# Cluster attention and a PReLU FFN on one core: copies of the queries' clusters, the table of weight conversions, and the turn back of the last batch are moved

## The chip, the cores and the metric

The kernel runs on one core of one Trainium2 chip. The time is device time in microseconds (us). A core has five engines that work side by side, each on its own queue in order: TensorE (PE, matmuls; its weight loads are PEld), VectorE (DVE), ScalarE (ACT), GpSimd (POOL) and SyncE (SP). Transfers (DMA) are issued by a queue, here mostly SP's, some by ScalarE's and GpSimd's, and then run by themselves. An instruction waits on semaphores that other engines or transfers raise.

## The reference

There are 4 batches of 8 heads with 768 tokens of 64 numbers. Each head has 16 centroids. Every query and every key goes to the centroid with which it has the largest cosine, and a query sees only keys of its own cluster. The result is put side by side over the heads and goes through a feed-forward network (FFN) of width 2048.

```python
q_assign = np.argmax(np.einsum('bhsd,hcd->bhsc', q_n, c_n), axis=-1)
k_assign = np.argmax(np.einsum('bhsd,hcd->bhsc', k_n, c_n), axis=-1)
mask = q_assign[:, :, :, None] == k_assign[:, :, None, :]
scores = np.where(mask, scale * np.matmul(q, k.transpose(0, 1, 3, 2)), -1000000000.0)
attn = softmax(scores)                       # over the keys
x = np.matmul(attn, v)                       # (B,H,S,D) -> (B*S, H*D), 3072 x 512
h = x @ w_in                                 # 512 x 2048
out = (np.maximum(h, 0.0) + alpha * np.minimum(h, 0.0)) @ w_out
```

The inputs q, k, v and the centroids are 32-bit floats; the weights of the FFN come to the chip as 64-bit floats, so the kernel converts them.

## The kernel before

**Tiles and steps.** Two heads are worked together as a pair; with four batches there are 16 pairs, pair n being heads 2hp and 2hp+1 of batch b, where n = 4b + hp. The 768 queries of a batch are cut into two halves of 384. In batches 0 to 2 the work of one pair and one half takes three steps, each with two blocks of 128 keys: so a batch has 24 steps, the first 12 for half 0 of its four pairs, the next 12 for half 1. The last batch (pairs 12 to 15) is sorted by cluster first and then needs only blocks near the diagonal.

**The order is written out by hand.** The loops over steps `u` emit the instructions of all engines, and each engine runs its own in that order. A step has five slots; `tick()` (L98) goes to the next slot and emits what `later(slots, piece)` (L95) had put there. Pieces can also be bound to a step and a slot through `at(step, slot, piece)` inside the loop that starts at L1072, run by `prepare(u, i)`. In slot 0 of a step come the scores and their exps (`score`, L735), in slot 1 the weighing with v (`weigh`) and the normalisation of a half that has ended; in slots 2 to 4 come FFN pieces (from step 12 on), preparations of later pairs, and one weight conversion per slot as long as `i < converting` (L1166). FFN pieces of a batch's half are fed in while the next half's attention runs.

**Clusters of batch 0.** For pair n, three steps ahead of its half 0, `prep_sims` multiplies features with centroids on TensorE, and `prep_argmax` (L414) makes on VectorE a one-hot table: the tile `member`, in which partitions 0 to 31 hold queries of half 0, 32 to 63 queries of half 1, and 64 to 127 the keys; a row is one of 2 x 16 clusters, a column a token. Seven slots later (twelve for pair 0) `of_heads` (L424) turns the keys' part into two masks, one per head, with two ScalarE passes (L426): a row of the head's own cluster becomes 0 for a key in it and -2^60 for others; rows of the other head become 0. Head 1's is written beside, head 0's in place of the one-hot table, so head 1's has to come first. In slot 2 of the step ahead of a half, `prep_queries` (L458) brings the queries' part to the partitions of the keys, into `aq`: by two copies on VectorE for the very first half (L469), and else by two transfers that ScalarE's queue issues (L471). In `score` two matmuls per head add mask times queries onto the scores (L763), head 0's first.

**Other work of ScalarE and VectorE in batch 0.** `prep_features` copies transposed features from PSUM to `qkT` on ScalarE (L358), three copies per pair, in the step ahead of `prep_sims`. The denominators of half 0 are summed by TensorE in one PSUM bank (L883); VectorE turns them (L896), inverts and spreads them (L902, L906, L865), and L990 writes the normalised result into `xT`, which frees the one PSUM bank of the weighing. L1014 is the first FFN matmul, over four channels, one for each pair's `xT`; L1032 is the second.

**Conversions.** There are 32, in four groups of four tiles of `w_in` and four of `w_out`, each of 128 x 512 numbers. `convert` (L244) issues the load into one of five raw buffers on SP's queue (L247) and gives three pieces. `split` is two VectorE instructions (L253, L255); four slots later `scale` is two on ScalarE (L259, L261); two slots later `join` is two on VectorE (L265, L268) and a product on GpSimd (L271). The tile `power` has three buffers. A raw buffer is loaded again when its join is done.

**The last batch's end.** `normalise_near` (L926) writes a pair's result in cluster order; it is turned to rows (L952, copied by ScalarE at L955), scattered back to token order by 12 indirect transfers that GpSimd issues (L960), and fetched by four transfers of SP (L972). Four slots after that has been issued, `turn_back` (L977) transposes the fetched rows into `xT` on VectorE (L982). Row sums of a pair's exps are made by additions (L815, L818), a turn (L824) and a sum (L832) on VectorE; L845 adds the parts up on TensorE. L795 applies masks on VectorE. L1006 is the slope of the PReLU on VectorE, after ScalarE's copy L1020. L696 and L702 prepare the next pair.

Of the kernel before, what the change touches and what calls it, by code (L numbers as in the profile page):

```python
# [11 lines left out]
BF16 = mybir.dt.bfloat16  # L12
# [3 lines left out]
AF = mybir.ActivationFunctionType  # L16
# [3 lines left out]
P = 128  # L20
# [3 lines left out]
def kernel(  # L24
# [11 lines left out]
    nc = tc.nc  # L36
# [5 lines left out]
    NCH = DM // P  # L42
    NF = DF // P
    HJ = NJ // 2
    HS = HJ * P
# [49 lines left out]
    def later(slots, piece):  # L95
        due.setdefault(now[0] + slots, []).append(piece)
# [317 lines left out]
    def prep_argmax(n, ps):  # L414
        top, first, pieces = argmax(ps, exact=n < NCH)
        for piece in pieces:
            piece()
        firsts[n] = first
        if n >= NCH:
            return  # L420
        member = memp.tile([P, 2, HS], BF16, name="member")
        nc.vector.transpose(out=member[:, 0, :], in_=top.rearrange("p t c -> p (t c)"))

        def of_heads():  # L424
            for h in (1, 0):
                nc.scalar.activation(  # L426
                    out=member[HP:P, h, :], in_=member[HP:P, 0, :], func=AF.Identity,
                    scale=pick[HP:P, h:h + 1], bias=pick[HP:P, h + 2:h + 3])

        members[n] = member  # L430
        later(12 if n == 0 else 7, of_heads)

    def prep_clusters(n):


        first = firsts.pop(n)
        ps = misc()
        for g in range(NG):
            nc.tensor.matmul(out=ps[:, g * 2 * NX:(g + 1) * 2 * NX], lhsT=spread[:, g, :],
                             rhs=first, start=True, stop=True)  # L440
        every = fsp.tile([P, NG, GT, NG, 2], BF16, name="every")
        everys[n] = every
        later(1, lambda: nc.scalar.copy(every.rearrange("p g i r h -> p (g i r h)"),
                                        ps[:, 0:NG * 2 * NX]))
        later(2, lambda: prep_keys(n))
# [12 lines left out]
    def prep_queries(n, half, h):  # L458

        if h == 0:  # L460
            aqs[n, half] = aqp.tile([P, 2, HS], BF16, name="aq")
        if n < NCH:

            if h == 0:
                r = slice(half * Q, (half + 1) * Q)
                for g in range(NG // 2, NG):
                    to = aqs[n, half][g * Q:(g + 1) * Q, 0, :]
                    if n == 0 and half == 0:
                        nc.vector.tensor_copy(out=to, in_=members[n][r, 0, :])  # L469
                    else:  # L470
                        nc.scalar.dma_start(out=to, in_=members[n][r, 0, :])  # L471
            return
        own_half = everys[n].rearrange("p g i r h -> p g (i r) h")[:, half, :, h:h + 1]
        nc.vector.transpose(out=aqs[n, half][:, h, :],
                            in_=own_half.broadcast_to((P, NX, Q)))
# [259 lines left out]
    def score(n, half, chunks, alone=None):  # L735


        qkT = qkTs[n]
        pss = [[ps_f.tile([P, 512], FP32, name="fps") for h in range(2)] if c == alone else
               ps_s.tile([P, 2, 512], FP32, name="sps") for c in chunks]  # L740
        early_mask = n < NCH

        def bank(ps, h, m=HS):
            return (ps[h] if isinstance(ps, list) else ps[:, h, :])[:, 0:m]

        def queries(c):
            lo, hi = ((half * HJ, (half + 1) * HJ) if half is not None else window(c))
            return slice(lo * P, hi * P), (hi - lo) * P

        for c, ps in zip(chunks, pss):  # L750
            tokens, m = queries(c)
            for h in range(2):
                r = h * D
                nc.tensor.matmul(  # L754
                    out=bank(ps, h, m),
                    lhsT=qkT[r:r + D, S + c * P:S + (c + 1) * P],
                    rhs=qkT[r:r + D, tokens], start=True, stop=not early_mask)
        if early_mask:
            for h in range(2):
                for c, ps in zip(chunks, pss):  # L760
                    g, i = divmod(NJ + c, GT)
                    r = slice(g * Q, (g + 1) * Q)
                    nc.tensor.matmul(  # L763
                        out=bank(ps, h), lhsT=members[n][r, h, i * P:(i + 1) * P],
                        rhs=aqs[n, half][r, 0, :], start=False, stop=True)
        for c, ps in zip(chunks, pss):
            E = e_tiles[0]
            e_tiles.append(e_tiles.pop(0))
            _, m = queries(c)
            if c == alone:  # L770
                for h in range(2):
                    nc.scalar.activation(out=E[:, h, 0:m], in_=ps[h][:, 0:m], func=AF.Exp,
                                         scale=SCALE)
            else:
                nc.scalar.activation(out=E[:, :, 0:m], in_=ps[:, :, 0:m], func=AF.Exp,  # L775
                                     scale=SCALE)
            waiting.append((n, half, c, E))
# [187 lines left out]
    def fetch_back(n, whole):  # L965

        b, hp = pairs[n]
        raw = inp.tile([P, 2, NJ, D], FP32, name="qk").rearrange("p h j d -> p (h j d)")
        for h in range(2):
            for x in range(D // Q):  # L970
                r = h * D + x * Q
                nc.sync.dma_start(  # L972
                    out=raw[r:r + Q, :].rearrange("p (t i) -> p t i", i=Q),
                    in_=whole[h * S:(h + 1) * S, x * Q:(x + 1) * Q].rearrange(
                        "(t p) i -> p t i", p=Q))

        def turn_back():  # L977
            for half in range(2):
                if (b, half) not in xTs:
                    pool = sorts["xmore"] if half else xpool  # L980
                    xTs[b, half] = pool.tile([P, NCH, HS], FP32, name="xT")
                nc.vector.transpose(out=xTs[b, half][:, hp, :],  # L982
                                    in_=raw[:, half * HS:(half + 1) * HS])
        later(4, turn_back)

    def normalise(n, half):
        b, hp = pairs[n]
# [84 lines left out]
    for (n, half), u in start_of.items():  # L1072
        def at(step, slot, piece):
            prep_at.setdefault((step, slot), []).append(piece)
        if half is None:
            t = ORDERS[n - NO]
            load_at.setdefault(t, []).append(lambda n=n: load(n))
            for i in range(2):
                at(t + 2, 2 + 2 * i, lambda n=n, i=i: order_features(n, i))
            at(t + 3, FIRST + 1, lambda n=n: order_sims(n))  # L1080
            at(t + 7, 2, lambda n=n: order_begins(n))
            load_at.setdefault(u - 4, []).append(lambda n=n: order_load(n))
            at(u - 4, 0, lambda n=n: prep_clusters(n))
            for i in range(2):
                at(u - 1, i, lambda n=n, i=i: order_blocks(n, i))
                at(u - 1, FIRST + i, lambda n=n, i=i: order_queries(n, i))
            continue
        if half == 0:
            if n < NCH:
                if n > 1:  # L1090
                    load_at.setdefault(max(u - 7, 0), []).append(lambda n=n: load(n))
                if n > 0:
                    load_at.setdefault(max(u - 6, 0), []).append(lambda n=n: load_v(n))
            else:
                load_at.setdefault(u - 9, []).append(lambda n=n: load(n))
                load_at.setdefault(u - 7, []).append(lambda n=n: load_v(n))
            if n < NCH:
                for g in range(len(groups)):
                    at(u - 4, FIRST + g, lambda n=n, g=g: prep_features(n, g))
            else:  # L1100
                for w in range(2):
                    at(u - 7, FIRST + w, lambda n=n, w=w: prep_blocks(n, w))
            at(u - (3 if n < NCH else 5 if u - 6 < TOGETHER else 6), FIRST,
               lambda n=n: prep_sims(n))
            if n >= NCH:
                at(u - 4, FIRST if u - 4 < TOGETHER else 0, lambda n=n: prep_clusters(n))
        for h in range(2):
            at(u - 1, FIRST + h, lambda n=n, half=half, h=h: prep_queries(n, half, h))

# [21 lines left out]
    for u in range(-AHEAD, TOGETHER):  # L1131
# [31 lines left out]
            feed_block(u)  # L1163
            whole = len(ffn) - KEEP
        take = (max(len(ffn) - KEEP - whole * (UB - 1 - u % UB) // UB, 0) if ffn else 0)
        converting = 0 if u < 0 else 2 if u < 2 else 1 + (u % 4 == 3) if u < UB else 2  # L1166
        for i in range(SLOTS - FIRST):
            tick()
            feed(take * (i + 1) // 3 - take * i // 3)
# [302 lines left out]
```

## Time and profile before

| what | value |
|---|---|
| median of 10 runs | 997.42 us (995.98 to 997.84) |
| profiled execution | 997.28 us |
| its span, first to last instruction | 995.4 us |
| TensorE busy | 970.3 us, 97% |
| VectorE busy | 634.4 us, 64% |
| up to 85.75 us: TensorE, VectorE, ScalarE busy | 75.45, 65.09, 52.87 us |
| 734.5 to 760.2 us: TensorE, VectorE busy | 22.12, 16.60 us of 25.70 |
| mean granted TensorE clock | 0.995 |

Batch 0's half 0 (steps 0 to 11) lasts to about 85.75 us, where the FFN begins beside the attention. In the views of the profile a row of a timeline is: start in us, length in us, engine, line, operation, what it writes `<-` what it reads, shapes, and how many instructions were merged; a bracket at its end gives the time for which its engine was idle before it and what ended that. The page's rows by slices cut the span into 40 equal parts, with the busy share of each in tenths. A table by stretch gives the length, then the busy time of PE, PEld, DVE, ACT and POOL (with instructions), the granted TensorE clock, the share of the DMA engines and GB/s.

### The profile page before, as it was taken

The page shows a single profiled execution, that of the slowest core. Times are in us where ns is not written, and L with a number is a line of the kernel's source. Part 1 is how long each engine was busy: PE and PEld are TensorE (multiplying, and loading weights), DVE is VectorE, ACT ScalarE, POOL GpSimd, SP SyncE. Part 2 cuts the span into 40 slices and gives each one's busy share as a digit, 9 for nine tenths or more (in the row PEclk, how much of TensorE's full clock was granted, in tenths as well). Part 3 has the DMA queues.
Part 4 walks back from the last instruction along what each step waited for, and adds up shares of the span by engine and source line. Part 5 has one row for each costly group of instructions (what it writes and reads, how often), then busy time and mean ns, then how long its engine had stood idle before and what let it go on. Part 6 is the DMA issues. An engine that isn't in the chain of part 4 may idle for free.

```text
span 995.4 us, 10857 instructions
## 1 busy us (share of the span) xinstructions
PE 970.3 (97%) x3947; PEld 481.3 (48%) x3947; DVE 634.4 (64%) x1143; ACT 258.3 (26%) x468; POOL 213.1 (21%) x249
## 2 busy tenths in 40 slices
PE   8899999999999999999999999999998999999997
PEld 5434444445454454545445454454554545455453
DVE  5887788598587776877857698678977522021010
ACT  5655443222121221212222022231222101010110
POOL 2322222010000635401000273620154440000000
PEclk9989999999999999999999999999999999999999
DMA  6533665042200362416020121811621120000000
GB/s 251 192 117 108 138 130 78 17 90 21 33 1 26 102 100 55 80 44 102 1 33 0 53 80 37 149 32 23 95 47 30 31 53 11 0 9 25 0 1 35
DMA packets 174285, 60.45 MB, mean 61 GB/s; under 512 B 161216, under 2 KB 164752, under 8 KB 174224
## 3 DMA queue, kind: packets, MB, share of 16 engines
q1 hardware_dynamic: 168768, 51.42, 24.2%
q0 software_dynamic: 4608, 7.87, 2.5%
q8 instruction: 33, 0.54, 0.2%
q10 hardware_dynamic: 848, 0.39, 0.2%
q14 instruction: 28, 0.23, 0.1%
HBM read 45.15 MB, written 14.16 MB: 60 GB/s over the span
## 4 chain that ended last, share of the span: by engine, by line
PE 90%; DVE 5%; ACT 2%; DMA 1%; issue 1%; POOL 0%; ACTq 0%; SPq 0%; DVEq 0%; POOLq 0%
PE fps L1014 32%; PE fps L1032 32%; PE vps L890 9%; PE sps L754 8%; PE fps L754 3%; PE sps L763 1%; PE mps L381 1%; ACT E L775 1%; DVE acc L824 1%; PE vps L923 1%; ACT member L426 1%; PE mps L923 1%; DVE gT L1006 1%; PE fps L883 0%; ACT power L259 0%
## 5 line engine op out<-in xcount | busy, mean ns | idle before, releaser
L1014 PE MATMUL fps<-xT,w_in_sb 128*128 128x384 f32 x1024 | 343.4, 491 | 2.7 <-ACT gT L1020 2.0
L1032 PE MATMUL fps<-w_out_sb,gT 128*128 128x512 f32 x768 | 341.2, 598 | 1.7 <-DVE gT L1006 1.7
L1014 PEld LDWEIGHTS fps<-xT,w_in_sb 128*128 128x128 f32 x1024 | 190.7, 190 | 142.8 <-ACT more L775 4.4
L1032 PEld LDWEIGHTS fps<-w_out_sb,gT 128*128 128x128 f32 x768 | 143.9, 191 | 174.3 <-issue 162.3
L660 POOL DMA_INDIRECT scratch<-stage,off x96 | 101.0, 1052 | 324.4 <-DMA stage<-in_v_dram 267.2
L1006 DVE SCALAR_TENSOR_TENSOR gT<-gT,alpha 128x384 f32<-128x384 f32 x128 | 80.8, 637 | 138.6 <-ACT gT L1020 138.3
L1020 ACT COPY gT<-fps 128x384 f32<-128x384 f32 x128 | 61.2, 478 | 337.8 <-PE fps L1014 335.7
L754 PE MATMUL sps<-qkT 64*128 64x384 f32 (+1 forms) x512 | 97.8, 501 | 0.6 <-ACT E L775 0.6
L795 DVE SCALAR_TENSOR_TENSOR more<-aq,key,more 128x384 f32<-128x384 bf16 (+1 forms) x136 | 74.4, 606 | 29.3 <-ACT more L775 19.0
L775 ACT ACTIVATE E<-sps 128x768 f32<-128x768 f32 (+1 forms) x81 | 61.2, 802 | 77.0 <-PE sps L763 45.7
L960 POOL DMA_INDIRECT back<-rows,place x48 | 49.6, 1034 | 103.6 <-ACT rows L955 90.2
L754 PEld LDWEIGHTS sps<-qkT 64*128 64x128 f32 x512 | 46.3, 189 | 46.4 <-issue 18.3
L890 PE MATMUL vps<-E,vt 128*64 128x384 f32 x356 | 67.0, 502 | 0.0
L795 DVE SCALAR_TENSOR_TENSOR E<-aq,key,E 128x384 f32<-128x384 bf16 (+1 forms) x104 | 56.5, 602 | 16.1 <-ACT E L775 11.4
L1040 DVE TENSOR_TENSOR y<-y,fps 128x512 f32<-128x512 f32 x30 | 20.6, 685 | 70.0 <-PE fps L1032 70.0
L805 DVE TENSOR_TENSOR acc<-acc,E 128x768 f32<-128x768 f32 x47 | 44.9, 956 | 16.9 <-ACT E L775 15.6
L1038 ACT COPY y<-fps 128x512 f32<-128x512 f32 x24 | 14.1, 586 | 144.2 <-PE fps L1032 144.2
L775 ACT ACTIVATE more<-sps 128x768 f32<-128x768 f32 (+1 forms) x47 | 35.4, 797 | 41.2 <-PE sps L754 40.8
L890 PEld LDWEIGHTS vps<-E,vt 128*64 128x64 f32 x356 | 23.3, 138 | 32.4 <-issue 31.7
L890 PE MATMUL vps<-more,vt 128*64 128x384 f32 x220 | 38.8, 491 | 0.0
L271 POOL TENSOR_TENSOR w_in_sb<-w_in_sb,power 128x512 f32<-128x512 f32 x16 | 22.2, 1385 | 71.1 <-DVE w_in_sb L268 71.1
L754 PE MATMUL fps<-qkT 64*128 64x384 f32 x160 | 34.5, 508 | 0.0
(177 smaller groups left out, 708.1 us busy)
## 6 DMA issues: line engine op xcount, KB each, us to landing
raw<-in_moe_w_in_dram SPq DMA_DIRECT2D x16, 512.0 KB, 4.2
raw<-in_moe_w_out_dram SPq DMA_DIRECT2D x16, 512.0 KB, 3.7
out_dram<-y SPq DMA_DIRECT2D x24, 256.0 KB, 2.1
vt<-in_v_dram SPq DMA_DIRECT2D x12, 384.0 KB, 4.3
qk<-in_q_dram SPq DMA_DIRECT2D x48, 96.0 KB, 3.5
qk<-in_k_dram SPq DMA_DIRECT2D x48, 96.0 KB, 3.5
qk<-scratch SPq DMA_DIRECT2D x32, 96.0 KB, 3.5
qk<-in_q_dram SPq DMA_DIRECT2D x4, 384.0 KB, 3.9
```

Of the source, the lines that this page charges most:

```text
L271: nc.gpsimd.tensor_tensor(out=dst, in0=dst, in1=power[0].bitcast(FP32), op=ALU.mult)
L660: nc.gpsimd.indirect_dma_start(out=scratch[n][1][h * NX + xx], out_offset=bass.IndirectOffsetOnAxis(ap=ranks[n][:, xx, h:h + 1], axis=0), ...
L754: nc.tensor.matmul(out=bank(ps, h, m), lhsT=qkT[r:r + D, S + c * P:S + (c + 1) * P], rhs=qkT[r:r + D, tokens], start=True, stop=not early_ ...
L775: nc.scalar.activation(out=E[:, :, 0:m], in_=ps[:, :, 0:m], func=AF.Exp, scale=SCALE)
L795: nc.vector.scalar_tensor_tensor(out=e, in0=of, scalar=keys[n][:, NJ + c, h:h + 1], in1=e, op0=ALU.is_equal, op1=ALU.mult)
L805: nc.vector.tensor_tensor(out=acc, in0=acc if first is None else first[3], in1=E, op=ALU.add)
L890: nc.tensor.matmul(out=po[r:r + D, 0:HS], lhsT=vts[n][:, h, c, :], rhs=e[:, h, :], start=(c == 0), stop=(c == NJ - 1))
L960: nc.gpsimd.indirect_dma_start(out=to[i], out_offset=bass.IndirectOffsetOnAxis(ap=place[:, h, j:j + 1], axis=0), in_=rows[:, j, h * D:(h + ...
L1006: nc.vector.scalar_tensor_tensor(out=gs[f], in0=gs[f], scalar=alpha[:, f:f + 1], in1=gs[f], op0=ALU.mult, op1=ALU.max)
L1014: nc.tensor.matmul(out=ps[:, 0:HS], lhsT=w_in_sb[:, c, f * P:(f + 1) * P], rhs=xTs[b, half][:, c, :], start=(c == 0), stop=(c == NCH - 1))
L1020: nc.scalar.copy(gs[f], ps[:, 0:HS])
L1032: nc.tensor.matmul(out=ps[:, 0:DM], lhsT=gs[f][:, i * P:(i + 1) * P], rhs=w_out_sb[:, f, :], start=on and f == f0, stop=off and f == f0 + ...
```

## The change

The one-hot table and the masks get tiles of their own: `member` keeps all of the table, and the two ScalarE passes write to a new tile `outside`, head 0 first. For pairs 1 to 3, the copies of half 0's queries are issued by `of_heads` itself, ahead of the two passes, at the start of the step before the half instead of in its slot 2. The copies of half 1 are issued three steps ahead of it instead of one. How many conversions begin in a step, which was 2, 2 and then 1, 2, 1, 1, 1, 2, 1, 1, 1, 2 for steps 0 to 11, comes from a table: 2, 0, 2, 2, 0, 2, 2, 1, 1, 1, 2, 2; the sum is 17 in both. `turn_back` follows nine slots after the fetch instead of four, but for the last pair.

```diff
-        member = memp.tile([P, 2, HS], BF16, name="member")
-        nc.vector.transpose(out=member[:, 0, :], in_=top.rearrange("p t c -> p (t c)"))
+        member = memp.tile([P, HS], BF16, name="member")
+        outside = memp.tile([P, 2, HS], BF16, name="outside")
+        nc.vector.transpose(out=member, in_=top.rearrange("p t c -> p (t c)"))

         def of_heads():
-            for h in (1, 0):
+            if n > 0:
+                prep_queries(n, 0, 0)
+            for h in range(2):
                 nc.scalar.activation(
-                    out=member[HP:P, h, :], in_=member[HP:P, 0, :], func=AF.Identity,
+                    out=outside[HP:P, h, :], in_=member[HP:P, :], func=AF.Identity,
                     scale=pick[HP:P, h:h + 1], bias=pick[HP:P, h + 2:h + 3])

-        members[n] = member
+        members[n] = member, outside
         later(12 if n == 0 else 7, of_heads)
...
                     if n == 0 and half == 0:
-                        nc.vector.tensor_copy(out=to, in_=members[n][r, 0, :])
+                        nc.vector.tensor_copy(out=to, in_=members[n][0][r, :])
                     else:
-                        nc.scalar.dma_start(out=to, in_=members[n][r, 0, :])
+                        nc.scalar.dma_start(out=to, in_=members[n][0][r, :])
...
-                        out=bank(ps, h), lhsT=members[n][r, h, i * P:(i + 1) * P],
+                        out=bank(ps, h), lhsT=members[n][1][r, h, i * P:(i + 1) * P],
...
-        later(4, turn_back)
+        later(4 if n == NP - 1 else 9, turn_back)
...
+        if n < NCH:
+
+            if half == 1 or n == 0:
+                at(u - (3 if half else 1), FIRST,
+                   lambda n=n, half=half: prep_queries(n, half, 0))
+            continue
         for h in range(2):
             at(u - 1, FIRST + h, lambda n=n, half=half, h=h: prep_queries(n, half, h))
...
-        converting = 0 if u < 0 else 2 if u < 2 else 1 + (u % 4 == 3) if u < UB else 2
+
+        converting = 0 if u < 0 else (2, 0, 2, 2, 0, 2, 2, 1, 1, 1, 2, 2)[u] if u < UB else 2
```

## The prediction

> **What bounds the kernel now.** The page first. TensorE is busy for 97% of a span of 995.4 us, so time can come only from its idle places, and the row of slices (40, digits in tenths) shows two: the first twelfth of the span, and a dent near 750 us.
>
> ```profile
> PE 970.3 (97%) x3947; PEld 481.3 (48%) x3947; DVE 634.4 (64%) x1143; ACT 258.3 (26%) x468; POOL 213.1 (21%) x249
> ...
> PE   8899999999999999999999999999998999999997
> ```
>
> Second, TensorE's timeline, where the square bracket is the idle time before a row and its releaser.
>
> ```profile
> 29.64 1.09 PE L354 MATMUL fps<-ident,qk 128*64 128x128 f32 x16 [1.76 <-ACT qkT L358]
> ...
> 48.65 1.21 PE L354 MATMUL fps<-ident,qk 128*64 128x128 f32 x16 [2.94 <-ACT qkT L358]
> ...
> 65.17 1.62 PE L754 MATMUL sps<-qkT 64*128 64x384 f32 x8 [0.60 <-ACT E L775]
> ...
> 68.48 0.85 PE L763 MATMUL sps<-aq,member 32*128 32x384 bf16 x4 [1.70 <-DMA aq<-member]
> ...
> 747.03 1.98 PE L1032 MATMUL fps<-w_out_sb,gT 128*128 128x512 f32 x4 [0.56 <-DVE gT L1006]
> 751.23 0.42 PE L845 MATMUL mps<-parts,fold 128*128 128x48 f32 x2 [2.21 <-DVE parts L832]
> 751.49 8.79 PE L1032 MATMUL fps<-w_out_sb,gT 128*128 128x512 f32 x16
> ```
>
> After the start-up (its last wait, 1.24 us, ends at 16.32) batch 0 has four waits: 1.76+2.94+0.60+1.70 = 7.00 us. The FFN's first L1014 begins at 85.75. The late dent has two: 0.56+2.21 = 2.77 us. Third, tables by stretch for the granted clock (the column before the DMA share):
>
> ```profile
> 49.50:53.00 3.50, 3.50 (x18) 1.31 (x13) 0.53 (x1) 0.58 (x1) 1.26 (x1) 0.51 0.58 211
> ...
> 70.00:73.40 3.40, 3.40 (x14) 1.27 (x12) 3.02 (x10) 1.86 (x4) 1.29 (x2) 0.50 0.80 263
> ...
> 752.60:756.10 3.50, 3.50 (x5) 1.35 (x5) 3.45 (x7) 0.00 (x0) 2.65 (x3) 0.51 0.10 33
> ```
>
> Behind three of the waits TensorE runs some 3.4 us at half clock, so each such wait costs about 1.7 us more. Last, VectorE's timeline in both places:
>
> ```profile
> 25.72 0.45 DVE L253 TENSOR_SCALAR power<-raw 128x512 uint32<-128x512 uint32 x1 [1.40 <-POOL w_in_sb L271]
> ...
> 31.57 1.76 DVE L268 SCALAR_TENSOR_TENSOR w_in_sb<-raw,w_in_sb 128x512 f32<-128x512 uint32 x1
> ...
> 739.40 1.04 DVE L982 STREAM_TRANSPOSE xT<-qk 128x384 f32<-128x384 f32 x2 [4.86 <-DMA qk<-back]
> ```
>
> At 739.40 the whole VectorE queue stood 4.86 us behind a turn back whose rows had not landed. The first row is a split that waits for GpSimd to free its power buffer; the second a join that takes 1.76 us instead of 0.69 because GpSimd's L271 runs from 31.13. The row that ends batch 0's half 0 on VectorE is L990 at 86.76, 0.56 long; the first FFN matmuls need its tile.
>
> **Turn back later.** For pairs 12, 13 and 14 the two transposes go five slots later in VectorE's queue; pair 15's stay. Nothing else on VectorE changes order there, and TensorE's and GpSimd's orders are the same throughout. For pair 12 the rows after the old place go on at 734.54 (end of the masks before it): two masks 1.02, two more 0.79, one slope 0.53 give 736.9; sums, turn and row sums of side 0 last 3.67 (742.70 to 746.37 now), giving 740.55; two slopes 1.05, whose second input ScalarE has by 740.63, give 741.6; three additions 1.79 give 743.4. Only now come the transposes: 0.96, to 744.4. Their data landed at 739.28, so they have 4.1 us to spare. Turn and row sums, 1.97, end at 746.3 instead of 751.18. TensorE's L1032 matmuls end at 746.47 and the slope they waited for is ready at 741.6: the 0.56 goes. The next four end at 748.5, L845's input is ready at 746.3: the 2.21 goes. The half clock goes with them: sixteen L1032 took 8.63 us on the chain against 6.97 at full clock elsewhere (167.60), 1.66. Sum 4.43 us. What is late next is ScalarE's copy of the hidden tile, waits of 0.24 to 0.57 that are there now too. Bounds: 2.2 if the clock or the 0.56 stays, 4.43 if all goes; I take 4.4, because the spare times are 2 to 5 us. Pair 13's transposes do not wait now (768.27); pair 14's 4.71 us at 791.25 is followed by slopes alone, and TensorE waits there only 0.24 and 0.57 for ScalarE: nothing gained. Who waits for the moved transposes? Only the last FFN blocks, from 824.8 us: nothing lost. SP's and GpSimd's queues are not passed by anything here; pair 13's scatter runs from 741.28 to 757.6 on GpSimd, with its gather about 7 us behind, before its new place near 772.
>
> [...]
>
> **The batch 0 edits.** Their order by engine: on ScalarE the copy pairs (0.5 to 0.6 us of issue each) move ahead of the two mask passes, pair 1's past six compute rows; four copies of half 1 come two steps earlier. No scale stands any more ahead of pair 2's three feature copies at 29.02, for step 1 has no conversions: that wait, 1.76, goes. SP issues pair 3's q and k ahead of two weight loads instead of behind: earlier, hidden. The separate mask tile lets head 0's matmuls start after one pass of 0.71, but head 1's need both, and the exp behind them waits for a feature copy until 16.84 anyway: 0, at most 0.2 gained.
>
> Then VectorE decides. Now it works from 33.51 (denominators of pair 0) to 87.32 (L990, pair 3), 53.81 us, with 4.08+0.20+0.18+1.10 = 5.56 idle: 48.25 of work. In the changed order the same stretch holds 13 splits and 13 joins instead of 12 and 11, because step 0's and 2's conversions slip behind it: one split 0.68 and two joins 2.40 more. Collisions with L271 (the second of two joins in a row, or the second half of a split that follows a join) are seven in both. Twice a split stands right behind the join whose GpSimd product must free its buffer; the rows of that are 1.40 and 1.38: 2.8. Sum 48.25+3.08+2.8 = 54.1. It starts 1.76 earlier, at 31.75, and ends at 85.9, or 86.5 if small gaps add up; now 87.32. TensorE, which by its own work reaches this point near 77.4 (87.75 less the four waits and two times 1.7), loses all that in other places: feature copies behind pair 2's scale, exps of step 8 behind scales that wait for splits, denominators and the vps bank waiting for VectorE. Those waits, and half clock behind them, lie beside VectorE's queue and cost nothing. The last one does not: the first hidden tile's fourth channel now starts at 87.75 (85.75 + 6 x 0.334); it would start near 86.2, 1.5 earlier, but after a wait of two to three microseconds, and half clock costs 1.7 there. Sum 0.2 lost. Bounds: 1.5 gained without that half clock; 3 lost with one more half-clock stretch on the path or one collision more (1.1). From step 12 on, 17 conversions are begun either way and the order is as before but for the copies.
>
> **Sum.** Against the profiled execution: 997.28 (span 995.40 and 1.88 around it) + 0.2 - 4.4 = 993.1. The median of the ten runs is 0.14 above that execution: 993.2.
>
> **Rivals.** *Batch 0 gains (13%).* All four waits and both half clocks vanish, 7.0+3.4: 982.6; with a third to a half of it 987 to 990. For: four of the edits take ScalarE's rows from in front of TensorE. Against: VectorE's 48 us of work in a stretch of 54 leave no room.
> *Batch 0 loses about 2.5 (13%).* One more half clock and a collision on the path: 995.7. For: VectorE has no slack from 32 to 86. Against: collisions are fixed by the order, which has as many.
> *Only part of the late wait goes (10%).* L845 comes without wait but the clock drops for other short waits there (0.57, 0.56): 995.4; if the turn back were not what held the queue, 997.6. Against: 4.86 us are named on it.
> *Slower (9%): copies hold ScalarE's queue.* In the built program each copy must first see an earlier transfer's counter; the half 1 copies see weight loads, which SP issues only when a buffer is free (four issues spread over 18.57 us at 50.06) and which land 3.7 to 4.2 us later. Issued two steps earlier, the copies at steps 9, 12, 15 and 18 could wait for loads that have not landed, with the exps behind them. Two full landings cost 8: 1001; it decides from 1.1 us of TensorE's wait per copy, where four take 4.4. Against: the copies of now look at such counters too, and TensorE's one wait for a copy, 1.70, came from a scale that waited for VectorE.
>
> **How the numbers follow.** My forecast has 55%, with its own range 991.8 to 994.8 (batch 0 from 1.3 gained to 1.5 lost). The range holds it, the two middle rivals and the upper half of the first: 989.5 to 997.3; left out are the far end of the first rival and the last. Two microseconds, 0.2%, is what a measurement can tell from no change. Faster by more: the forecast, the first rival, half of the second and third, 0.79. Within: 0.13. Slower: 0.08.
>
> **What would show it.** Right: the turn back at 739 has moved behind three additions without idle time before it, L845 and the L1032 before it start without waits, and no half clock follows. Right also: TensorE's wait for pair 2's features at 28 us is gone, VectorE idles there instead, then stays busy to 86, and TensorE waits in batch 0 name VectorE or an exp, the last on L1014 for xT. Wrong: L1014 starting well before 84, TensorE waiting on a copy at steps 9 to 18, or the dent at 750 still there.

## The result: 991.74 us, and the profile after

The changed kernel takes 991.74 us (median of 9 runs, 991.3 to 994.44); the kernel before, beside it, 997.39 us (median of 30, 995.42 to 997.87). The ratio is 0.9957, 95% interval 0.9948 to 0.9965. The profiled execution took 992.54 us, span 990.7 us against 995.4.

In the page of the changed kernel TensorE is busy for 967.9 us against 970.3 (most of the difference is one half-clock stretch less, 3.41 us at a granted clock of 0.50), and in the row of slices the dent near 750 us is gone, the one at the start is not. Lines from L430 on now have numbers 3 higher (L754 is L757, L982 is L985, L1032 is L1035, and so on).

```profile
PE 967.9 (98%) x3947; PEld 480.6 (49%) x3947; DVE 633.1 (64%) x1143; ACT 259.3 (26%) x468; POOL 215.1 (22%) x249
...
PE   8988999999999999999999999999999999999997
```

TensorE's timeline of the changed kernel, in batch 0 and behind 741 us:

```profile
45.35 1.09 PE L354 MATMUL fps<-ident,qk 128*64 128x128 f32 x16 [1.77 <-ACT qkT L358]
...
62.08 2.00 PE L757 MATMUL sps<-qkT 64*128 64x384 f32 x8 [2.41 <-ACT E L778]
...
71.27 1.51 PE L893 MATMUL vps<-E,vt 128*64 128x384 f32 x8 [0.67 <-DVE xT L993]
...
86.20 7.74 PE L1017 MATMUL fps<-xT,w_in_sb 128*128 128x384 f32 x18 [2.99 <-DVE xT L993]
...
741.25 7.13 PE L1035 MATMUL fps<-w_out_sb,gT 128*128 128x512 f32 x16
748.22 0.32 PE L848 MATMUL mps<-parts,fold 128*128 128x48 f32 x2
748.38 7.10 PE L1035 MATMUL fps<-w_out_sb,gT 128*128 128x512 f32 x16
```

The waits of 1.76 us at 28 us, 1.70 us for a copy, and 0.56 and 2.21 us near 750 us are gone. In their place batch 0 has one of 2.41 us behind an exp and one of 2.99 us behind VectorE, just before the first hidden tile's fourth channel. The waits of batch 0 shown above add up to 7.84 us, where the kernel before had 7.00. On VectorE the late turn back now stands behind the additions, without a bracket:

```profile
742.83 0.69 DVE L821 TENSOR_TENSOR acc<-acc,more 128x512 f32<-128x512 f32 x1
743.44 1.03 DVE L985 STREAM_TRANSPOSE xT<-qk 128x384 f32<-128x384 f32 x2
...
745.36 0.95 DVE L835 TENSOR_REDUCE parts<-acc 128x24 f32<-128x768 f32 x1
```

So the two profiles differ by this: step 13's scores start at 93.87 us instead of 93.69 (0.18 lost in batch 0); at 740 us the changed kernel is still 0.19 behind; the scores that follow the late dent start at 755.41 instead of 760.21, so 4.99 us are won there.

### The profile page after: what moved, and what is told of

Read it like the earlier page. It is cut to its first block, busy times and chain, and to the rows that moved or that the text cites. A ratio compares the mean times of both kernels' runs of the same rounds, so it can differ in the third digit from the quotient of the medians.

```text
span 990.7 us, 10869 instructions
## 1 busy us (share of the span) xinstructions
PE 967.9 (98%) x3947; PEld 480.6 (49%) x3947; DVE 633.1 (64%) x1143; ACT 259.3 (26%) x468; POOL 215.1 (22%) x249
## 4 chain that ended last, share of the span: by engine, by line
PE 91%; DVE 6%; ACT 1%; issue 1%; POOL 1%; ACTq 0%; DVEq 0%; POOLq 0%
PE fps L1017 33%; PE fps L1035 33%; PE vps L893 8%; PE sps L757 8%; PE fps L757 3%; PE mps L381 1%; PE vps L926 1%; PE mps L926 1%; PE sps L766 1%; DVE power L265 1%; ACT gT L1023 1%; PE fps L354 0%; DVE w_in_sb L268 0%; PE vps L201 0%; PE mps L848 0%
## 5 line engine op out<-in xcount | busy, mean ns | idle before, releaser
L1035 PE MATMUL fps<-w_out_sb,gT 128*128 128x512 f32 x768 | 339.2, 596 | 1.1 <-DVE gT L1009 1.1
L1035 PEld LDWEIGHTS fps<-w_out_sb,gT 128*128 128x128 f32 x768 | 143.4, 190 | 172.3 <-issue 161.9
L757 PE MATMUL sps<-qkT 64*128 64x384 f32 (+1 forms) x512 | 96.5, 495 | 2.4 <-ACT E L778 2.4
L757 PEld LDWEIGHTS sps<-qkT 64*128 64x128 f32 x512 | 45.6, 186 | 47.1 <-issue 17.4
L271 POOL TENSOR_TENSOR w_in_sb<-w_in_sb,power 128x512 f32<-128x512 f32 x16 | 26.1, 1633 | 73.8 <-DVE w_in_sb L268 73.8
L757 PE MATMUL fps<-qkT 64*128 64x384 f32 x160 | 34.5, 508 | 0.0
```

What stands on the lines that cost most here:

```text
L271: nc.gpsimd.tensor_tensor(out=dst, in0=dst, in1=power[0].bitcast(FP32), op=ALU.mult)
L757: nc.tensor.matmul(out=bank(ps, h, m), lhsT=qkT[r:r + D, S + c * P:S + (c + 1) * P], rhs=qkT[r:r + D, tokens], start=True, stop=not early_ ...
L1035: nc.tensor.matmul(out=ps[:, 0:DM], lhsT=gs[f][:, i * P:(i + 1) * P], rhs=w_out_sb[:, f, :], start=on and f == f0, stop=off and f == f0 + ...
```

## The experiments

The runs fell on three chips, here the first, second and third, each with the kernel before beside them; times are compared within one chip. All results, as medians:

| edit | chip | time, us | kernel before, us | ratio, 95% interval |
|---|---|---|---|---|
| late turn back alone | first | 995.47 | 996.16 | 0.9991, 0.9982 to 1.0 |
| batch 0 edits alone | first | 997.09 | 996.16 | 1.001, 1.0001 to 1.0019 |
| table alone | first | 995.67 | 996.16 | 0.9993, 0.9984 to 1.0002 |
| copies and mask tile alone | first | 994.7 | 996.16 | 0.9984, 0.9975 to 0.9993 |
| changed kernel without table | second | 990.94 | 996.25 | 0.9945, 0.9932 to 0.9959 |
| changed kernel | second | 992.88 | 996.25 | 0.9964, 0.995 to 0.9977 |
| changed, lighter table | second | 990.09 | 996.25 | 0.9936, 0.9922 to 0.9949 |
| late turn back alone | third | 995.4 | 996.96 | 0.9985, 0.9976 to 0.9994 |
| changed kernel | third | 995.13 | 996.96 | 0.9989, 0.998 to 0.9998 |
| changed, pair 12 alone late | third | 995.74 | 996.96 | 0.9988, 0.9979 to 0.9997 |
| changed, smooth table | third | 988.54 | 996.96 | 0.9918, 0.9904 to 0.9931 |

### The parts alone

The turn back alone, in the kernel before:

```diff
-        later(4, turn_back)
+        later(4 if n == NP - 1 else 9, turn_back)
```

> The kernel before with one edit, the turn back of pairs 12 to 14 queued nine slots after the last score instead of four. Theory (the two parts of the change are independent, and nearly all of the gain is the turn back): 4.4 to 5.0 us less than the kernel before, about 992.5 to 993; TensorE's waits of 0.56 and 2.21 us near 750 us gone, no half clock there; batch 0 as in the kernel before, with its four waits and the first hidden tile's fourth channel at about 87.7 us. Rival (the batch 0 edits carry a part of the gain, and the late part is smaller than the one profile says): 2.2 to 3.5 us less, 994 to 995.2.

Measured: 0.7 us less, far under the theory and under the rival, and not told from no change (the interval reaches 1.0). TensorE's waits near 750 us were gone as expected; they can't have cost much on this chip.

The batch 0 edits alone, in the changed kernel:

```diff
-        later(4 if n == NP - 1 else 9, turn_back)
+        later(4, turn_back)
```

> The changed kernel with the old turn back (four slots): the batch 0 edits alone. Theory (VectorE's queue decides where batch 0 ends, so that the waits which go are replaced by others): the same as the kernel before within 1.7 us (one half-clock stretch more or less), centre +0.2; step 13's scores within 0.5 us of the kernel before; both late waits near 750 us, 0.56 and 2.21 us, are there with their half clock. Rival (batch 0 gains on its own): 2 us or more faster. Rival (the copies queued earlier hold ScalarE): 1.5 us or more slower with TensorE waiting on an exp behind a copy at steps 9 to 18.

Measured: 0.93 us slower, within the theory's bounds, with three half-clock stretches in the profiled execution (mean clock 0.994; behind waits of 1.75 and 2.42 us eight scores take 2.78 and 2.93 us instead of 1.56, behind one of 3.00 us 17 hidden-tile matmuls 7.27, where 18 take 6.04 with the copies alone) and no wait on a copy. Two expectations failed. Step 13's scores came at 95.61 us in that execution, not within 0.5 us of the 93.69 of the kernel before. And the late waits, which were to be there unchanged, were not: L848 waited 1.04 us once, without half clock (the sixteen L1035 behind it last 7.10 us).

The table alone (the edit is shown), and its counterpart, the changed kernel with the old count of conversions and the old turn back:

```diff
-        converting = 0 if u < 0 else 2 if u < 2 else 1 + (u % 4 == 3) if u < UB else 2
+        converting = 0 if u < 0 else (2, 0, 2, 2, 0, 2, 2, 1, 1, 1, 2, 2)[u] if u < UB else 2
```

> The kernel before with the table of conversions alone (2 0 2 2 0 2 2 1 1 1 2 2 in place of 2 2 1 2 1 1 1 2 1 1 1 2): copies and the mask tile as before, old turn back. Theory: TensorE's wait of 1.76 us for pair 2's features at 28 us goes already by the table, since it is the scale of step 1's conversions that stood ahead of them; the two waits near the copies (2.94 and 1.70 us) stay in some form; VectorE's queue is as full as in the changed kernel and ends the half 0 product of pair 3 at 85.5 to 87.5 us; time within 2 us of the kernel before. Rival (the copies are what matters in batch 0): the wait at 28 us stays.

> The changed kernel with the old count of conversions per step and the old turn back: the mask tile of its own and the copies issued early, alone. Theory: TensorE's wait of 1.76 us for pair 2's features stays, the wait of 1.70 us for a copy of queries' clusters goes; VectorE's queue is untouched, so that the half 0 product of pair 3 still ends at about 87.3 us, and the time is that of the kernel before within 2 us. Rival (the copies hold ScalarE's queue): 1.5 us or more slower. Rival (the copies were on the path): 1.7 us or more faster.

Measured: the table alone can't be told from the kernel before; the wait at 28 us went, its last product L990 ended at 86.77 us, and TensorE waited for copies four times in batch 0's half 0, 2.48 us together. The copies alone took 1.46 us off; the wait at 28 us stayed (1.70 us), that for a copy went, and nothing held ScalarE's queue. VectorE's last product ended at 85.70 us, not 87.3, but the kernel before has it at 87.32 in one of its profiles and at 86.36 in the other, so most of that is not the edit's. The late wait (L845, here L848) was 1.25 us with the table alone and 1.11 us with the copies alone, without half clock (7.10 us for the sixteen matmuls behind it in both). VectorE's rows show why it was so short, here with the copies alone:

```profile
734.08 0.56 DVE L932 TENSOR_TENSOR qk<-vps,rd 128x384 f32<-128x384 f32 x1 [3.81 <-PE sps L757]
...
738.45 1.04 DVE L985 STREAM_TRANSPOSE xT<-qk 128x384 f32<-128x384 f32 x2 [2.23 <-DMA qk<-back]
```

VectorE stood 3.81 us for TensorE's scores before it came to the turn back, where 2.23 us were left of the 4.86. (In the first profile of the kernel before it stood 0.35 and 0.71 us there instead: the sum of its waits is 5.92 and 6.04 us, nearly the same.) In all four profiles of this chip TensorE takes some 1.05 us longer near 632 us and 1.8 us longer near 733 us than in the profiles of before and after. New theory: the gain of the late turn back depends on where TensorE stands when the rows land.

### The same kernels on another chip, without the table, and with less of it

> The changed kernel itself, on the chip of these runs. In the four runs of single parts TensorE takes 1.05 us longer than in the profiles before and after at 632 us and 1.8 us longer at 733 us, in the scores of L754, without a wait that the profile names, and the late wait is 1.0 to 1.25 us without half clock. Theory (the gain of the late turn back depends on where TensorE stands against the landing of the turned rows: a TensorE that comes later by 2.8 us had nothing to wait for): with those two delays present the changed kernel gains only 0.5 to 2 us over the kernel before here, and without them 4.5 to 5.7 again. Rival (the two parts help only together): 4.5 to 5.7 us faster also with the two delays present.

> The kernel before itself, for its profile beside the others of this call. Theory: where TensorE's scores at 632 and 733 us are delayed by 1.05 and 1.8 us, the turn back at 739 us waits 2.2 to 2.4 us instead of 4.86 and L845 waits 1.0 to 1.3 us instead of 0.56 and 2.21 with half clock. Rival: the waits of 4.86, 0.56 and 2.21 us and the half clock near 750 are there as in the first profile, with or without the delays.

Neither profile of the second chip has the two delays, and most of the gain is back: 992.88 against 996.25, 3.37 us, though the theory said 4.5 to 5.7. In the one execution of the kernel before that was profiled (996.42 us) the turn back waits 4.96 us and TensorE 0.65 and 2.22 us, with half clock (8.79 us for the sixteen L1032 behind it). TensorE's timeline of the kernel before on this chip, and of the changed one:

```profile
740.11 5.41 PE L1032 MATMUL fps<-w_out_sb,gT 128*128 128x512 f32 x12
746.18 1.98 PE L1032 MATMUL fps<-w_out_sb,gT 128*128 128x512 f32 x4 [0.65 <-DVE gT L1006]
750.38 0.42 PE L845 MATMUL mps<-parts,fold 128*128 128x48 f32 x2 [2.22 <-DVE parts L832]
750.64 8.79 PE L1032 MATMUL fps<-w_out_sb,gT 128*128 128x512 f32 x16
759.37 1.35 PE L754 MATMUL sps<-qkT 64*128 64x256 f32 x8
```

```profile
741.19 7.13 PE L1035 MATMUL fps<-w_out_sb,gT 128*128 128x512 f32 x16
...
755.34 1.35 PE L757 MATMUL sps<-qkT 64*128 64x256 f32 x8
```

From the L1032 row to the next scores it is 19.26 us before and 14.15 after: 5.11 us, as in the first pair of profiles. Up to there the changed kernel is 1.08 us behind, probably with more half clock by then: its mean clock is 0.995 without any in the late place, that of the kernel before 0.996 with a stretch there. That, and some 0.5 us behind 790 us, is what the theory's 4.5 to 5.7 lacks.

The changed kernel without its table, the `converting` line as before:

> The changed kernel without its table: copies, mask tile and late turn back, conversions counted as in the kernel before. Theory (the parts add up, and the table is the part of the batch 0 edits that costs): the copies alone took 1.5 us off the kernel before and the turn back alone 0.7, together 2.2: some 994, and faster than the changed kernel on the same chip by what the table costs, 1 to 2.4 us. Rival (the table pays in the changed kernel, and its cost in the run of batch 0 alone was the clock): not faster than the changed kernel.

Measured: 990.94 us, 1.94 less than the changed kernel here, all five executions at 990.11 to 991.66 (those of the changed kernel 991.27 to 994.48). (The 994 of the expectation took the first chip's 0.7 us for the turn back.) So beside the copies the table costs, on this chip and on the first (997.09 with both, 994.7 with the copies alone: 2.39 us). By itself it cost nothing (995.67 against 996.16): the two edits do not simply add up. TensorE's waits without the table:

```profile
30.18 1.09 PE L354 MATMUL fps<-ident,qk 128*64 128x128 f32 x16 [1.71 <-ACT qkT L358]
...
49.35 1.09 PE L354 MATMUL fps<-ident,qk 128*64 128x128 f32 x16 [3.09 <-ACT qkT L358]
...
65.36 1.62 PE L757 MATMUL sps<-qkT 64*128 64x384 f32 x8 [1.68 <-ACT E L778]
...
73.27 1.51 PE L893 MATMUL vps<-E,vt 128*64 128x384 f32 x8 [0.93 <-DVE xT L993]
...
85.86 4.43 PE L1017 MATMUL fps<-xT,w_in_sb 128*128 128x384 f32 x13 [0.65 <-DVE xT L993]
```

Their sum is 8.06 us; with the table it is 8.31 (0.50+1.75+2.40+0.67+2.99). VectorE ends its last product at 85.72 us without the table and at 86.00 with it. What differs is how the idle time is spread: the table saves TensorE's early waits, so it arrives early at the place that VectorE decides, and idles there 2.99 us in one piece, behind which it works at half clock (0.50 from 87.07 us in its first profile). Without the table no stretch of batch 0's half 0 behind the start-up is at half clock in the profiled execution (mean clock 0.999, the rows of eight scores 1.56 to 1.62 us). 0.28 us earlier and 1.7 us of half clock saved make the 1.98 us by which TensorE is ahead afterwards (at 200.72 instead of 202.70 us in the same wait of 0.86 us).

VectorE relieved before that place:

```diff
-(2, 0, 2, 2, 0, 2, 2, 1, 1, 1, 2, 2)[u]
+(2, 0, 2, 2, 0, 2, 2, 1, 1, 1, 0, 0)[u]
```

> The changed kernel with no conversions begun in steps 10 and 11 (the table ends in 0 0 instead of 2 2; the four are begun later). Theory (VectorE's queue sets the end of batch 0): the half 0 product of pair 3 comes 2 to 4 us earlier, TensorE's wait of 2.99 us before the first hidden tile shrinks to under 1 us and the half clock behind it goes, 2 to 4.5 us faster than the changed kernel on the same chip. Rival (the work only moves behind step 12 and is paid there, or another engine ends the stretch): within 1 us of the changed kernel.

Measured: the median is 2.79 us less than the changed kernel's, the profiled execution 4.92 (987.9 against 992.82 us); the other four took 989.92 to 990.2, for which no profile says why. VectorE's timeline, and TensorE's first hidden tile:

```profile
73.55 0.71 DVE L268 SCALAR_TENSOR_TENSOR w_out_sb<-raw,w_out_sb 128x512 f32<-128x512 uint32 x1
79.64 0.38 DVE L899 STREAM_TRANSPOSE simT<-fps 128x192 f32<-128x192 f32 x1 [5.39 <-PE fps L886]
...
81.96 0.56 DVE L993 TENSOR_TENSOR xT<-vps,rd 128x384 f32<-128x384 f32 x1
```

```profile
80.95 8.01 PE L1017 MATMUL fps<-xT,w_in_sb 128*128 128x384 f32 x24
```

Four conversions fewer, and VectorE waits 5.39 us for TensorE; its product comes at 82.51 instead of 86.00 and the 24 matmuls run through. So VectorE's queue, its waits for GpSimd's products included, sets the end of batch 0 in the changed kernel: TensorE's wait names its product, and in its rows from 52 to 86 us VectorE stands idle for nothing but three of these products (1.37, 1.18 and 1.39 us). The conversions put off were not paid later: TensorE is 4.87 us ahead of the changed kernel at 197.83 us and 4.86 ahead at 766.35.

### The third chip: once more, pair 12 alone, and a smooth table

> The turn back alone once more, the same kernel as in the first run of it, since the chip of that run delayed TensorE's scores at 632 and 733 us in every kernel. Theory (the late turn back is worth 4.4 to 5 us where TensorE isn't delayed there, and about 1 where it is): without the two delays in this profile 3.8 to 5 us faster than the kernel before, with them 0.5 to 1.5. Rival (the two parts of the change help only together): under 2 us also without the delays.

> The changed kernel on the chip of these runs, to stand beside the turn back alone: what it takes more or less than that is the batch 0 edits. Theory (+0.2 us for the batch 0 edits, with one half-clock stretch of 1.7 us more or less by the execution): within 1.7 us of the turn back alone. Rival (the batch 0 edits carry a part of the gain): 2 us or more faster than the turn back alone.

This chip has the two delays again, in all four profiles. The turn back alone gains 1.56 us and the changed kernel 1.83, so the batch 0 edits add nothing that can be told. Both theories hold within the noise, the first by its branch with delays (0.5 to 1.5 us). The delay in TensorE's timeline of the changed kernel, on the second chip and then on the third:

```profile
732.05 0.92 PE L757 MATMUL fps<-qkT 64*128 64x384 f32 x4
732.80 1.24 PE L757 MATMUL sps<-qkT 64*128 64x384 f32 x8
733.97 2.85 PE L1017 MATMUL fps<-xT,w_in_sb 128*128 128x384 f32 x8
```

```profile
731.91 0.91 PE L757 MATMUL fps<-qkT 64*128 64x384 f32 x3
733.44 0.48 PE L757 MATMUL fps<-qkT 64*128 64x384 f32 x1 [0.61 <-issue]
733.45 2.44 PE L757 MATMUL sps<-qkT 64*128 64x384 f32 x8
735.82 2.85 PE L1017 MATMUL fps<-xT,w_in_sb 128*128 128x384 f32 x8
```

The same twelve matmuls last 1.92 us and 3.91 us, with nothing named that they wait for. The turn back alone was not run on a chip without the delays; what it brings there is read from the two pairs of profiles (4.99 and 5.11 us), and from the table at the end of this section.

Pair 12 alone late, in the changed kernel:

```diff
-        later(4 if n == NP - 1 else 9, turn_back)
+        later(9 if n == NO else 4, turn_back)
```

> The changed kernel with the turn back of pair 12 alone at nine slots, those of pairs 13 and 14 at four as in the kernel before. Theory (only pair 12's had work behind it that TensorE waited for): the same time as the changed kernel within 0.5 us; pair 14's transposes wait some 4.7 us again at 787 us and no TensorE wait over 0.7 us follows. Rival (pair 14's wait cost too): 1 us or more slower than the changed kernel.

Measured: 0.61 us more at the median, a little over the 0.5 of the theory, but the executions differ by half clock; the two at a mean clock of 0.997 took 994.55 and 994.73 us, those of the changed kernel 994.69 to 995.02. Pair 14's transposes waited 2.52 us at 791.35 us, not 4.7, and TensorE's waits behind them were 0.24 and 0.57 us for ScalarE's copies, as in the changed kernel. From the scores behind the dent to the hidden tile after pair 14 it is 31.06 us (760.18 to 791.24), in the changed kernel 31.05 (757.19 to 788.24). So pair 12 carries it; the times alone could not tell, for the whole is small on this chip.

The smooth table:

```diff
-(2, 0, 2, 2, 0, 2, 2, 1, 1, 1, 2, 2)[u]
+(2, 0, 2, 2, 0, 1, 1, 1, 1, 1, 1, 0)[u]
```

> The changed kernel with the table 2 0 2 2 0 1 1 1 1 1 1 0: as many conversions less as the lighter table has more than none in steps 10 and 11, and nowhere two in a step from step 5 on. Theory (two conversions in a step make splits wait for GpSimd and joins run beside it; VectorE stood idle for 5.4 us before step 12 in the lighter table, so there is room for one): TensorE's waits at 62 and 71 us, 2.4 and 0.7 us with a half clock, shrink, no wait before the first hidden tile over 0.7 us; 0 to 3 us faster than the lighter table, 986 to 990 where the kernel before takes 996.3. Rival (the waits at 62 us come from ScalarE's own queue): they stay, and the time is that of the lighter table.

Measured: 988.54 us (988.05 to 989.61), 6.6 less than the changed kernel and 8.4 less than the kernel before on this chip: the best of all by its ratio. TensorE's waits in batch 0's half 0 after the start-up are two, and its first hidden tile begins 3.0 us before the lighter table's on the second chip:

```profile
45.30 1.09 PE L354 MATMUL fps<-ident,qk 128*64 128x128 f32 x16 [1.75 <-ACT qkT L358]
...
61.31 1.62 PE L757 MATMUL sps<-qkT 64*128 64x384 f32 x8 [1.69 <-ACT E L778]
...
77.96 8.01 PE L1017 MATMUL fps<-xT,w_in_sb 128*128 128x384 f32 x24
```

In the changed kernel on this chip TensorE waits 2.39 us at 62 us, 1.70 at 72 us and 1.42 before the first hidden tile's fourth channel. The first became 1.69, the others went, and no stretch of half 0 behind the start-up is at half clock (mean clock 0.999, the rows of eight scores 1.56 to 1.62 us). This fits the theory that with one conversion per step fewer scales on ScalarE wait for a split ahead of an exp: in the changed kernel a scale that waited 2.23 us for its split (start 58.82 us) stands ahead of the exp that TensorE waits for, in the smooth table none.

But the smooth table also begins fewer conversions in batch 0: 12, where the lighter table begins 13 (not as many, as was written) and the changed kernel 17. How much of the 6.6 us is the even spread, and how much the five conversions less, no run separates; the lighter table was not run on this chip. A small part is paid later: the wait at 195.62 us is 1.69 us instead of 0.86. The two delays are in this profile too; on a chip without them the kernel was not run.

Three lengths read from the rows of all 14 profiles put the parts side by side. The first is the start of step 13's scores, which tells what batch 0 took; the second goes from there to the first L1032 near 740 us, and shows the two delays; the third goes from that L1032 to the next scores, the place of the late dent.

| kernels (profiles) | step 13's scores, us | to the late L1032, us | late place, us |
|---|---|---|---|
| before, first measurement and second chip (2) | 93.69, 92.73 | 647.4 | 19.15, 19.25 |
| changed, first measurement and second chip (2) | 93.87, 93.81 | 647.4 | 14.15 |
| changed without table, second chip (1) | 91.84 | 647.4 | 14.15 |
| changed, lighter table, second chip (1) | 88.89 | 647.4 | 14.15 |
| late turn back alone, first and third chip (2) | 93.92, 93.23 | 650.2, 650.1 | 14.15 |
| batch 0 edits alone, table alone, copies alone, first chip (3) | 95.61, 93.49, 91.82 | 650.2 | 15.46, 15.67, 15.53 |
| changed, and pair 12 alone late, third chip (2) | 92.60, 95.80 | 650.4, 650.2 | 14.15 |
| changed, smooth table, third chip (1) | 85.90 | 651.1 | 14.15 |

With pair 12's turn back late, the late place takes 14.15 us in all nine profiles, whatever was done in batch 0. With the old one it takes 19.2 without the delays and 15.5 to 15.7 with them: the turn back is worth 5.0 to 5.1 us or 1.3 to 1.5. So the rival that the two parts help only together is not what the late place shows.

## Why the prediction was right, and what it owed to the chip

993.2 us were forecast with 989.5 to 997.3 around it; 991.74 came, 1.5 less. The profiled execution is nearer: 992.54 us, where the sum for it was 993.1. It has a mean clock of 0.995, the median execution one of 0.997, which is about one half-clock stretch (1.7 us) less.

**Turn back.** Its steps hold to some two tenths: the transposes were to be reached at 743.4 us and came at 743.44 without a wait, the parts were to be ready at 746.3 and were (745.36 + 0.95), the waits of 0.56 and 2.21 us and the half clock went. Two terms were too small: 4.99 us came for 4.43 (4.4 in the sum). From the first L1032 to L845 it is 10.17 us before and 6.97 after, 3.20 where the brackets say 2.77: each of the two waits cost some 0.2 us that stands in no bracket. In the rows of TensorE, four L1032 behind a wait last 1.98 us, where sixteen without one last 7.13, which is 1.78 for four; why, no row shows. And the half clock gave 1.79 (8.98 from L845 to the next scores before, 7.19 after) instead of 1.66. The stalls of pairs 13 and 14 were rightly costed at nothing.

**Batch 0.** The sum of +0.2 us came as +0.18, and the way there was the one foreseen: VectorE's stretch from the denominators to the last product ran from 31.38 to 86.06 us, forecast 31.75 to between 85.9 and 86.5; then came a wait of 2.99 us ("two to three microseconds") with half clock on the path (0.50 from 87.07 to 90.48 us). The half clock behind the wait at 62 us (0.50 from 63.18 to 66.60 us) lay beside VectorE's queue, as was said of such. Not right: that the stretch would be 51.33 us of work, with seven collisions, and 2.8 us of waits for GpSimd. Of the 54.68 us measured, four such waits are 5.10 (1.16, 1.38, 1.17 and 1.39 us), and 49.58 are left for the work, with five collisions (rows of some 1.5 or 1.76 us); the errors, 2.3 us up and 1.75 down, nearly cancelled. Nor do all of TensorE's waits in batch 0 name VectorE or an exp: that of 1.77 us at 45 us names a feature copy. That the number itself fits is luck: step 13's scores, by which the 0.18 is read, start at 92.60 to 95.80 us in the five profiles with all batch 0 edits and at 92.73 to 93.92 in the four with none. And as one lump the edits hid two that oppose each other, copies that gain (1.46 us alone on the first chip) and a table that costs beside them (1.94 us on the second, 2.39 on the first).

**The rivals.** That copies queued earlier hold ScalarE didn't come true in any run. In all nine profiles with the early copies no wait of ScalarE and none of TensorE names a transfer of queries' clusters, while in all five without them TensorE waits for one. The rival in which batch 0 gains was wrong for this change, but more than the third to a half of it that the prediction priced is to be had: on the third chip the same matmuls start at 202.11 us with batch 0 as before (the late turn back alone) and at 195.62 with the smooth table. VectorE has to be relieved for it, which its "against" had said.

**What one profile couldn't say.** The terms of the turn back are differences between a landing and TensorE's arrival. They were right where TensorE was not delayed (the first pair of profiles and the second chip) and about three times too large on the first and third chips (1.3 to 1.5 us by the rows for 4.43; 0.69 and 1.56 us by the medians). There TensorE came 2.8 to 3.0 us later, and in the kernels with the old turn back that were profiled, on the first chip, 1.0 to 1.25 us of the wait was left, without half clock. The times fit this: the kernel before is hardly slower on these chips (996.16 and 996.96 us, 996.25 on the second), for the delays eat a wait that it has anyway; the changed kernel is slower (995.13 us on the third, 992.88 on the second). That the measurement fell on a chip without them was luck: on the third chip the changed kernel gained 1.83 us (0.9989), and there the step that fails is what of the wait lies on the path, not the mechanism.

**The clock.** The prediction charged 1.7 us to "such a wait", one of 1.70 to 2.94 us. The runs show it behind some waits of this size and not behind others: 2.94 us of idle time cost no clock in the late turn back alone on the third chip, nor did 3.09 us in the changed kernel without its table. The last section has them side by side.

## What to carry to other kernels

A wait that a shared in-order engine takes for a transfer is worth moving behind work that others wait for (here 5.0 to 5.1 us, and 1.3 to 1.5 where TensorE came later); its price is the difference of two arrival times, so look whether a second chip has the same difference. Where an engine's queue decides the end of a stretch, saving the other engine's earlier waits only collects them in one piece at the end (here 2.99 us): take work out of the deciding queue. Less of it, spread one piece per step, was the best run here, though what the spread alone brings was not separated. Judge edits that oppose each other singly and in pairs: the table that cost 2 us beside the copies cost nothing alone.

## What the runs showed of the hardware

**Half clock behind waits.** In the first profiles of before and after, each half-clock stretch behind a wait lasts 3.41 us at a granted clock of 0.50: from 49.49, 69.97 and 752.64 us before, from 63.18 and 87.07 us after. In the 3.41 us ahead of them TensorE had idled 2.57, 1.76 and 2.01 us before, 2.31 and 2.54 us after. Tables by stretch, first of the changed kernel and then of the late turn back alone on the third chip; the second number is TensorE's busy time, and the granted clock stands behind the five engines:

```profile
83.66:87.07 3.41, 0.87 (x3) 0.64 (x4) 3.15 (x10) 0.00 (x0) 0.90 (x1) 1.00 0.46 154
87.07:90.48 3.41, 3.41 (x7) 1.73 (x6) 2.25 (x5) 0.48 (x1) 1.57 (x1) 0.50 0.23 53
```

```profile
45.00:48.41 3.41, 1.75 (x33) 1.51 (x28) 3.41 (x6) 3.33 (x5) 1.87 (x2) 1.00 0.44 107
48.41:51.83 3.42, 2.14 (x24) 1.54 (x24) 2.65 (x4) 2.30 (x5) 1.85 (x2) 1.00 0.70 217
51.83:55.24 3.41, 3.41 (x40) 1.17 (x36) 1.49 (x8) 2.50 (x4) 0.58 (x1) 1.00 0.54 161
```

In the first, 2.54 us idle are followed by half clock. In the second, 1.66 and 1.28 us idle, 2.94 together, are followed by a clock of 1.00; in the kernel before a wait of the same 2.94 us, in its first profile, was followed by half clock. Nor does the length of a wait tell it elsewhere. A wait of 1.75 us at 45 us was followed by half clock in the batch 0 edits alone (the eight scores behind it take 2.78 us) and not in the smooth table (1.56 us). The 1.70 us for a copy in the kernel before were followed by it at 69.97 us; 1.70 us at 28 us with the copies alone were not, nor 3.08 us at 49 us there, nor 3.09 us at 49 us without the table (1.56 us for the scores behind each). The 2.41 us at 62 us in the changed kernel were followed by it at 63.18 us, the 1.69 us that the smooth table left there were not (1.62 us). What decides it these runs don't show. It differs between executions of one kernel too: the changed kernel's times in its first measurement lie near 991.5, 993 and 994.4 us, at mean clocks of 0.997, 0.995 and 0.993.

**Two delays without a name.** On two of the three chips of the experiments, in all eight profiles, TensorE takes about 1.05 us longer near 632 us and 1.7 to 2.0 us longer near 733 us, with the scores of L754; on the second chip, and in the first profiles of before and after, it does not. The table above has both together as 2.8 to 3.0 us in its second length (647.4 against 650.1 to 650.4). At 733 us the idle time is put down to issue; at 632 us to an exp that itself starts at 632.85, 1.7 us after the records have its scores end (changed kernel, third chip). The granted clock is 1.00 in both places. What delays TensorE there stays open.
